# A recurrent-attention and FFT-gate kernel: hand-ordered chunk pipeline, natural-layout output, bonus summed on VectorE, half-length inverse, one PSUM ring

## The chip, the cores and the metric

The kernel runs on one core of a Trainium2 chip. Time is device microseconds (us) of one execution. Engines are named as in the profile: PE (TensorE matmul; PEld is its weight load), DVE (VectorE), ACT (ScalarE), POOL (GpSimd), SP (SyncE, which here only issues DMAs). SBUF and PSUM are the two on-chip memories in which the kernel keeps its tiles; its matmuls all write to PSUM tiles. The granted clock is the share of its full clock at which the profile shows PE running. Medians come from a few timed executions. Every run has a state, fast or slow.

## The reference, cut to what matters

Part one is a recurrence over 768 time steps for each of 4 batches and 8 heads of 48 channels. Part two projects its output, convolves one third of it with a filter by FFT, multiplies it by two gates and projects again.

```python
for t in range(S):                                    # S = 768, D = 48
    cur = einsum('bhd,bhe->bhde', u[None] * kt, vt)   # the "bonus"
    y[:, :, t] = einsum('bhd,bhde->bhe', rt, state + cur)
    state = wt[..., None] * state + einsum('bhd,bhe->bhde', kt, vt)
# x = y as (B, S, 384)
proj = x @ w_proj;  x1, x2, x3 = three parts of 384
x2_conv = irfft(rfft(x2, axis=1) * rfft(filter_fft, axis=0), n=S, axis=1)
return (x1 * x2_conv * x3) @ w_out
```

## The kernel before

Time is cut into chunks of 128 steps: 6 a batch, 24 in all. A chunk turns the recurrence into matmuls: cumulative sums of log decay (`csi`, `csT`), scaled keys `kh` and queries `qT`, scores `sc`, a masked score `mt`, the state, and the output `yT`, which is built channel-first. Two half sums `sd` of each pair of chunks (from chunk 3 of a batch on) feed the transform. The second stage of a batch (gates, transform, spectrum products, inverse, output projection) is a queue of closures, let in three at a time between the parts of later chunks. The framework's scheduler then orders each engine.

```python
# part_b: bonus on PE, from transposed r*k (tkT's second half)
for x, o in ((kh, 0), (rk, HP)):
    for j in range(HP):
        nc.tensor.transpose(tk[:, o + j, :], x[:, 2*j:2*j+2, :], ident)
nc.scalar.activation(out=tkT, in_=tk, func=AF.Copy)
...
nc.tensor.matmul(kv[:, C+2*j:C+2*j+2], tkT[:, HP+j, :], u_sb[:, j, :], ...)
...
nc.vector.tensor_copy(out=cc, in_=kv[:, C:])
nc.vector.tensor_mul(mt, sc..., mask)
nc.gpsimd.tensor_mul(vc, v_heads(vb), cc.to_broadcast(...))

# second stage: spectrum products on VectorE, six operations on 128x1152
def prods():
    nc.vector.tensor_mul(ua, xr, HR);  nc.vector.tensor_mul(ub, xi, HI)
    nc.vector.tensor_sub(pr, ua, ub)
    nc.vector.tensor_mul(ua, xr, HI);  nc.vector.tensor_mul(ub, xi, HG)
    nc.vector.tensor_add(pi, ua, ub)

# inverse: six full matmuls for each of 3 blocks x 2 halves
def inv(cb, hf):
    for n, q in enumerate((0, 2, 4, 1, 3, 5)):
        m = m2n[:, q-2, :] if (hf and q >= 2) else m2[:, q, :]
        nc.tensor.matmul(ps, P[q % 2][:, q//2, cb*L:(cb+1)*L], m, ...)
    nc.vector.tensor_mul(y[:, cb, sl], ps, g[:, cb, sl])
```

## Time and profile before

| | before |
|---|---|
| time, median | 222.61 us (221.51 to 223.82) |
| span of the profiled execution | 222.3 us |
| start to the first half sums | 48.8 us |
| three periods from batch to batch | 46.5, 46.4, 46.4 us |
| last first-half-sums to the end (tail) | 34 us |

The start time of the first half sums `sd` of each batch is the marker used all through; it cuts the run into a head, three periods and a tail. These lines are from the page of the profile: busy time by engine; in 40 slices the granted PE clock and the DMA share, in tenths; and the chain of work that ended last.

```profile
span 222.3 us, 4668 instructions
...
PE 181.1 (81%) x1778; PEld 123.3 (55%) x1778; DVE 143.8 (65%) x260; ACT 124.1 (56%) x233; POOL 81.6 (37%) x129
...
PEclk9999559699999999999999999999999999999998
DMA  6999999939598244995950709987401041000022
...
PE 53%; DVE 20%; ACT 12%; DMA 6%; issue 6%; SPq 1%; POOL 1%; DVEq 0%; ACTq 0%; POOLq 0%
```

No engine is full, and the chain passes through several. The same kernel by stretches of time (from and to, length, then busy time and instructions by engine, granted clock, DMA share, GB/s):

```profile
48.79:95.31 46.52, 41.72 (x437) 28.62 (x434) 32.81 (x53) 28.15 (x55) 18.74 (x29) 1.00 0.72 146
95.31:141.68 46.37, 41.55 (x437) 28.78 (x434) 32.30 (x54) 28.21 (x55) 18.07 (x29) 1.00 0.63 129
...
188.20:222.30 34.10, 25.14 (x193) 14.29 (x191) 15.19 (x28) 13.92 (x27) 2.45 (x3) 0.97 0.10 36
```

In a period DVE is busy 32 us of 46 (third pair of numbers), ACT 28, POOL 18. In the chain of waits (start, us, what), the head has one long piece:

```profile
10.52 11.23 DMA r_84<-in_r_dram
...
21.91 0.73 POOL rk_93 L321
22.86 0.84 POOL vc L364
```

POOL, which works in order, waits for chunk 2's `r` before it makes chunk 0's `vc`. Three groups by form (busy us, mean ns):

```profile
L490 DVE TENSOR_TENSOR y<-ps_i,g 128x384 bf16<-128x384 f32 x24 | 12.8, 555 | 16.5 <-PE ps_i L485 16.5
...
L456 DVE TENSOR_TENSOR sd_1437<-xT_841 128x384 bf16<-128x384 bf16 x3 | 3.4, 1127 | 1.7 <-ACT xT_841 L403 1.7
...
L456 DVE TENSOR_TENSOR sd_2907<-xT_2325 128x384 bf16<-128x384 bf16 x3 | 1.6, 521 | 2.7 <-ACT xT_2325 L403 2.7
```

The half sum has both inputs in SBUF and takes 1.13 us in batch 1, where POOL is at work, and 0.52 us in the last batch, where it nearly rests.

### The profile page before, as it was taken

Reading aid. Unit: us, or ns where it says so; the run is one execution under the profiler, and the core shown is the slowest. Engines: PE = TensorE matmul, PEld = TensorE weight load, DVE = VectorE, ACT = ScalarE, POOL = GpSimd, SP = SyncE. Lnnn points to the kernel's source line nnn. Section 1 sums busy time; section 2 is a strip of 40 time slices with the busy share of each in tenths; the row PEclk is TensorE's granted clock in tenths of the full one; section 3 lists DMA queues with packets and bytes.
Section 4 is the critical chain, followed back from the end, with each engine's and each line's share of the span. In section 5 each row is a group of like instructions: output and inputs, shape, how many; then the busy total and the mean of one; then the engine's idle time right before and its main releaser. Section 6 shows DMA issues by size and latency. Waiting matters only on the chain.

```text
span 222.3 us, 4668 instructions
## 1 busy us (share of the span) xinstructions
PE 181.1 (81%) x1778; PEld 123.3 (55%) x1778; DVE 143.8 (65%) x260; ACT 124.1 (56%) x233; POOL 81.6 (37%) x129
## 2 busy tenths in 40 slices
PE   0066797988798999978898999887979999779882
PEld 0054555766555657666465666665656666645341
DVE  8946366387759845776679384786696537734730
ACT  2396447467676346576773445767842475656022
POOL 8740366447312433463423235363232432400000
PEclk9999559699999999999999999999999999999998
DMA  6999999939598244995950709987401041000022
GB/s 132 175 307 229 282 166 193 182 66 198 108 192 158 56 85 100 257 179 112 174 108 2 143 19 278 173 170 137 79 3 35 0 147 69 4 0 0 3 106 108
DMA packets 105863, 27.44 MB, mean 123 GB/s; under 512 B 100464, under 2 KB 105456, under 8 KB 105840
## 3 DMA queue, kind: packets, MB, share of 16 engines
q1 hardware_dynamic: 105040, 25.96, 54.7%
q0 software_dynamic: 800, 1.18, 3.1%
q8 instruction: 14, 0.23, 0.5%
q14 instruction: 9, 0.07, 0.1%
HBM read 23.59 MB, written 4.72 MB: 127 GB/s over the span
## 4 chain that ended last, share of the span: by engine, by line
PE 53%; DVE 20%; ACT 12%; DMA 6%; issue 6%; SPq 1%; POOL 1%; DVEq 0%; ACTq 0%; POOLq 0%
PE yT L400 10%; PE ps_p L431 9%; PE ps_i L485 9%; DMA r_84<-in_r_dram 5%; PE ps_o L495 4%; DVE mt L362 4%; PE ps_f L254 3%; PE rT L317 3%; PE ps_f L246 3%; PE sc L355 3%; DVE g L443 2%; ACT tkT L337 2%; DVE sd_1437 L456 2%; DVE sd_2179 L456 2%; DVE sd_695 L456 2%
## 5 line engine op out<-in xcount | busy, mean ns | idle before, releaser
L362 DVE TENSOR_TENSOR mt<-sc,mask_excl 128x1024 bf16<-128x1024 f32 x24 | 29.2, 1216 | 1.1 <-PE sc L355 1.1
L337 ACT ACTIVATE tkT<-tk 128x1024 bf16<-128x1024 bf16 x24 | 24.6, 1023 | 1.4 <-PE tk L335 1.2
L490 DVE TENSOR_TENSOR y<-ps_i,g 128x384 bf16<-128x384 f32 x24 | 12.8, 555 | 16.5 <-PE ps_i L485 16.5
L431 PEld LDWEIGHTS <-wproj 128*128 128x128 bf16 x144 | 13.4, 99 | 14.1 <-issue 6.9
L499 ACT ACTIVATE o<-ps_o 128x384 f32<-128x384 f32 x24 | 11.4, 493 | 15.8 <-PE ps_o L495 15.8
L318 ACT ACTIVATE csi<-csi 128x384 f32<-128x384 f32 x24 | 11.6, 482 | 13.8 <-PE csi L310 13.8
L360 DVE COPY cc<-kv 128x8 f32<-128x8 f32 x24 | 3.9, 164 | 23.0 <-PE kv L347 22.8
L400 PE MATMUL yT<-ident,vc 128*128 128x128 bf16 x72 | 16.2, 225 | 2.2 <-POOL vc L364 2.2
L495 PE MATMUL ps_o<-wout,y 128*128 128x384 bf16 x72 | 15.2, 326 | 1.3 <-DVE y L490 0.7
L364 POOL TENSOR_TENSOR vc<-v_87,cc 128x384 bf16<-128x384 bf16 x8 | 6.6, 830 | 16.3 <-DVE cc L360 16.2
L272 PE MATMUL m2t<-ident,F 128*128 128x128 bf16 x18 | 2.8, 305 | 11.5 <-DVE ident L190 11.5
L324 DVE TENSOR_TENSOR qT<-rT,e_96 128x512 bf16<-128x512 f32 x12 | 8.2, 687 | 5.0 <-ACT e_96 L319 5.0
L355 PE MATMUL sc<-qT,tkT 48*128 48x128 bf16 x192 | 11.3, 223 | 0.0
L321 POOL TENSOR_TENSOR rk_93<-r_84,ld_k 128x384 bf16<-128x384 f32 x6 | 6.0, 999 | 13.1 <-PE tk L335 7.0
L400 PE MATMUL yT<-qT,st_98 128*128 128x128 bf16 x72 | 9.9, 219 | 0.7 <-DVE kh_91 L322 0.6
L368 POOL TENSOR_TENSOR phi<-e_95,blk 128x8 f32<-128x8 f32 x12 | 2.9, 244 | 20.4 <-ACT e_95 L319 17.3
L495 PEld LDWEIGHTS <-y 128*128 128x128 bf16 x72 | 6.6, 97 | 6.7 <-DVE y L490 1.9
L254 PE MATMUL ps_f<-ab,F 128*128 128x384 bf16 x48 | 9.7, 327 | 0.2
L400 PE MATMUL yT<-mt,v_87 128*128 128x128 bf16 x80 | 8.9, 219 | 1.1 <-DVE mt L362 1.1
L364 POOL TENSOR_TENSOR vc<-v_86,cc 128x384 bf16<-128x384 bf16 x8 | 6.6, 831 | 8.2 <-DVE cc L360 8.2
L400 PE MATMUL yT<-mt,v_88 128*128 128x128 bf16 x80 | 8.7, 225 | 0.8 <-DVE mt L362 0.8
L324 DVE TENSOR_TENSOR qT<-rT,e_95 128x512 bf16<-128x512 f32 x12 | 8.2, 684 | 1.4 <-ACT e_95 L319 1.2
(278 smaller groups left out, 538.4 us busy)
## 6 DMA issues: line engine op xcount, KB each, us to landing
ld_w<-in_w_dram SPq DMA_DIRECT2D x24, 192.0 KB, 3.9
ld_k<-in_k_dram SPq DMA_DIRECT2D x24, 192.0 KB, 3.2
ld_v<-in_v_dram SPq DMA_DIRECT2D x24, 192.0 KB, 4.2
out_dram<-o SPq DMA_DIRECT2D x3, 1152.0 KB, 5.2
filt<-in_moe_filter_fft_dram SPq DMA_DIRECT2D x2, 1152.0 KB, 8.2
r_82<-in_r_dram SPq DMA_DIRECT2D x6, 192.0 KB, 4.0
r_83<-in_r_dram SPq DMA_DIRECT2D x6, 192.0 KB, 3.6
r_84<-in_r_dram SPq DMA_DIRECT2D x6, 192.0 KB, 4.0
```

The source lines that it names most:

```text
L254: nc.tensor.matmul(ps, F[:, ti, c0:c0 + L], x[:, ti, :], start=(ti == 0), stop=(ti == NT - 1),)
L324: nc.vector.tensor_mul(qT, rT, e[:, :, 0:L])
L337: nc.scalar.activation(out=tkT, in_=tk, func=AF.Copy)
L355: nc.tensor.matmul(sc[:, par, j, :], tkT[p0:p0 + D, j, :], qT[p0:p0 + D, j, :], start=True, stop=True,)
L362: nc.vector.tensor_mul(mt, sc.rearrange("p q j t -> p (q j) t"), _mid(mask_excl, H))
L364: nc.gpsimd.tensor_mul(vc, v_heads(vb), cc.to_broadcast([L, H, D]))
L400: nc.tensor.matmul(yT[:, cb, :], lh, rh, start=(n == 0), stop=(n == len(ops) - 1))
L431: nc.tensor.matmul(ps, wproj[:, cb, col0:col0 + L], xT[:, cb, sl], start=(cb == 0), stop=(cb == CB - 1),)
L456: nc.vector.tensor_add(z(f"sd{0}")[:, :, sl], lo, hi)
L485: nc.tensor.matmul(ps, z(f"P{q % 2}")[:, q // 2, cb * L:(cb + 1) * L], m, start=(n == 0), stop=(n == 5),)
L490: nc.vector.tensor_mul(z("y")[:, cb, sl], ps, z("g")[:, cb, sl])
L495: nc.tensor.matmul(ps, z("y")[:, cb, ti * L:(ti + 1) * L], wout[:, cb, :], start=(cb == 0), stop=(cb == CB - 1),)
```

## The change

The intent: fewer and smaller matmuls, kept in an order made by hand. The bonus sum `cc` becomes a reduction on DVE of a product made by POOL; `kh` moves from DVE to POOL; the chunk's output is built time-first and then transposed; the inverse computes even and odd parts of half length, which DVE adds and subtracts; all PSUM tiles but the scores share one ring of six; the filter is loaded and transformed later.

```diff
+    def bonus_a(idx):
+        nc.gpsimd.tensor_mul(rk, r_bufs[idx % NR][:, :, 0:D], t["lk"])
+        nc.gpsimd.tensor_mul(t["rku"], rk, u_bc)
+        nc.gpsimd.tensor_copy(out=t["vb"], in_=t["lv"])
+    def bonus_b(idx):
+        nc.vector.tensor_reduce(out=cc, in_=t["rku"], axis=AX.X, op=ALU.add)
+        nc.gpsimd.tensor_mul(t["vc"], t["vb"], cc.to_broadcast([L, H, D]))
...
-        nc.vector.tensor_mul(kh[:, :, 0:D], lk, csi)
+        nc.gpsimd.tensor_mul(kh[:, :, 0:D], t["lk"], en)
...
-        def inv(cb, hf):            # 6 full matmuls, 6 times a batch
+        def inv(cb):                # 4 full, 4 half-row matmuls, 3 times
+            full = ((0, 0, 0, ev), (1, 1, 0, ev), (4, 0, 2, od), (5, 1, 2, od))
+            ...                     # first P0's, then P1's slices
+            nc.scalar.activation(out=ods, in_=od, func=AF.Copy)
+            nc.vector.tensor_add(eo[:, 0, :], ev, ods)
+            nc.vector.tensor_sub(eo[:, 1, :], ev, ods)
+            nc.vector.tensor_mul(z("y")[:, cb, :], eo..., z("g")[:, cb, :])
...
+    FILL = (2, 2, 2, 0)             # units of side work a chunk lets in
+    with tc.manual_schedule(engines={PE, Activation, DVE, Pool, SP}):
+        for idx in range(len(chunks)):
+            turn(idx)                          # transpose kh
+            begin(idx + 2); load_weights(idx); issue_loads(idx + 4)
+            fill(FILL[0])
+            scores(idx); decay(idx + 1); bonus_b(idx + 1); bonus_a(idx + 2)
+            fill(FILL[1])
+            output(idx)
+            fill(FILL[2])
+            turn_x(idx, xTs[b])                # transpose the output
...                                            # side work of batches 0 to 2:
+            ready[5] += fws + [F(prods, slice(0, 3))]
+            ready[5] += g1[0:4] + invs[0:1] + g1[4:6] + invs[1:3]
```

In the last batch the products are made in three slices between the transform's steps. The output steps of a batch are put into the queue in chunk 3 of the next. A unit is one queued step; an inverse block counts as two, the products and the half sums as none.

## The prediction

> **What bounds the kernel now.** No engine is full: the page has PE at 81% of 222.3 us, DVE 65%, ACT 56%, POOL 37%. The chain of waits gives PE 53%, DVE 20%, ACT 12%. I read three stages. (a) Head, to 48.8 us (first half-sums, group `sd`): the windows have the DMA share at about 1.0 until 40 us, and the chain has one wait of 11.2 us for chunk 2's `r`, because POOL's product for chunk 2 stands before chunk 0's `vc`. (b) Three batch periods of 46.4 us (`sd` at 48.8, 95.3, 141.7, 188.2). DVE is busy 32.5 us in each, ACT 28.1, POOL 18. PE reads 41.6, but that holds pipeline latency: in the timeline a run of six 384-column matmuls takes 1.14 us and one 0.33, so the step is 0.16 us; 128 columns 0.056, a concurrent half-row matmul 0.091, scores 0.025. With these steps a batch needs about 37 us of PE, 79% of the period; the rest is hand-offs (score, mask, `yT`, `xT`, `sd` in turn on the chain). (c) Tail, 34 us, of which 25 follow the last chunk.
>
> **Costs of the change, per batch.**
> PE: the inverse goes from 36 full matmuls to 12 full and 12 concurrent halves: 5.8 to 3.0 us. A chunk drops four `rk` transposes, four bonus products, and 19 `yT` steps of 0.056 us for 13 mostly small ones, and adds three transposes and one identity product: 2.75 to about 2.25 us. Together 37 to about 31 us.
> DVE: `kh` (0.55 us a chunk) goes to POOL, `cc` (0.16) becomes a reduction over 384 elements, which I estimate at 0.55. The Trainium skill ("VectorE: DVE Perf Modes", the perf-mode tier table) gives a reduction only the plain rate, like the 0.55 us of the 384-element tensor-tensors here. The inverse's six 0.55 us become six of 0.55 and three of about 0.55: +1.7. Net about +1: 33 to 36.5 us.
> ACT: the key transpose halves (1.02 to about 0.59), `xn` adds 0.49, `ods` 1.5 a batch: about 32 us.
> POOL: about 4.4 us a chunk instead of 3.4.
> The skill ("SBUF — State Buffer", on the shared port pair) says a two-input VectorE operation from SBUF waits for a GpSimd operation reading SBUF. The trace agrees: `sd` takes 1.13 us on average in busy batches, 0.52 in the last. More POOL work keeps that cost.
>
> So the bound moves to DVE, 36-37 us a batch. PE's saving (6 us) counts only because the order made by hand lets hand-offs overlap.
>
> **On the critical path.** Batch period 46.4 to about 41 (DVE near 88%): about 16 us over three. Head: POOL's wait goes, the 3.7 us of zeroing before the masks go, the filter load moves back; but chunk loads (about 4.7 us of all DMA engines each) still pace it: 4-6 us. Tail: shorter inverse, products by slice, outputs after: about 6 us; the last inverse's chain (copy, add, subtract, multiply, about 2.2 us) gives some back.
>
> **Predicted: 193 us**, 184 to 204 in 8 of 10. Faster by over 2%: 0.94; within: 0.04; slower: 0.02.
>
> **What would show it.** DVE's busy share near 75%, PE's falling to about 75% with about 1490 matmuls; POOL above 50%; batch period 40-42 us; no DMA wait over 5 us on POOL in the head; inverse matmuls about 1 us a block; half-sums not faster than before.
>
> **What would make it wrong.** ACT, issuing in order, waits for a late `w` load before the chunk's own work, so the head stays DMA-paced; key product on POOL (1 us, late) holds the transposes; DVE blocked longer by POOL; one PSUM ring of six holding PE. Then 200-210. If hand-offs vanish and DVE runs above 93%: 182.

## The result and the profile after

The changed kernel took 204.02 us (median of 202.74 to 206.22), beside 223.22 us for the kernel before in the same rounds. The ratio, 0.913 with a 95% interval of 0.904 to 0.922, is the mean time of the one kernel's fast runs over that of the other's of the same rounds, so it is not quite the ratio of the medians. All ratios below are made that way against the kernel before. The result lies at the very end of the stated range (184 to 204), 11 us above the number predicted.

| | before | predicted | after |
|---|---|---|---|
| start to first half sums | 48.8 us | 43 to 45 | 39.7 us |
| periods | 46.5, 46.4, 46.4 | 41 each | 46.7, 40.8, 40.9 us |
| tail | 34 | 28 | 34.7 us |

The page of the changed kernel, as above:

```profile
span 202.9 us, 4168 instructions
...
PE 156.5 (77%) x1490; PEld 97.7 (48%) x1490; DVE 153.6 (76%) x249; ACT 126.5 (62%) x269; POOL 121.6 (60%) x162
...
PEclk9999696996999969999999799999997999999678
DMA  6999989799987871833989928339930000140024
...
DVE 31%; PE 25%; issue 12%; ACT 12%; DMA 8%; SPq 6%; POOL 4%; DVEq 0%; ACTq 0%; POOLq 0%
```

DVE now leads the chain. The granted clock has a dip in every batch and a long one at the end, which the kernel before did not have after its head. By stretches:

```profile
39.70:86.45 46.75, 37.73 (x388) 23.98 (x387) 41.42 (x57) 30.17 (x67) 33.26 (x39) 0.93 0.85 150
86.45:127.26 40.81, 35.27 (x363) 22.36 (x362) 36.67 (x51) 28.48 (x65) 29.75 (x37) 0.96 0.73 146
...
168.16:202.90 34.74, 26.11 (x171) 12.86 (x169) 19.33 (x44) 17.38 (x38) 3.02 (x5) 0.89 0.19 69
```

DVE is busy 36.7 us of 40.8, POOL 29.7 where it was 18. The groups that answer to those shown of before:

```profile
L483 DVE TENSOR_TENSOR y<-eo,g 128x768 bf16<-128x768 bf16 x12 | 14.0, 1164 | 0.4
...
L436 DVE TENSOR_TENSOR sd_1353<-xT_866 128x384 bf16<-128x384 bf16 x3 | 2.9, 962 | 0.0
...
L435 DVE TENSOR_TENSOR sd_1351<-xT_866 128x384 bf16<-128x384 bf16 x3 | 1.6, 523 | 2.0 <-ACT xT_866 L385 2.0
```

The new gate product `y` has both inputs in SBUF. The 1.16 us is a mean over all twelve: the three of the last batch, where POOL is idle, take 0.56 us each, and the nine of the other batches 1.28 to 1.41, 1.37 on average.

The most telling view is the timeline of one batch (start us, us, engine, line, what; in brackets the idle time before it and what ended it). These lines are cut out of the stretch from 103 to 115 us:

```profile
103.07 1.23 DVE L343 TENSOR_TENSOR mt<-sc,mask_excl 128x1024 bf16<-128x1024 f32 x1 [1.99 <-PE sc L338]
...
105.81 0.75 DVE L455 TENSOR_TENSOR U_1805<-X_1684,HR 128x1152 bf16<-128x1152 bf16 x1
106.47 1.39 DVE L456 TENSOR_TENSOR U_1806<-X_1690,HI 128x1152 bf16<-128x1152 bf16 x1
107.21 1.51 POOL L280 TENSOR_TENSOR rk<-r_76,ld_k 128x384 bf16<-128x384 f32 x1
107.89 1.44 DVE L457 TENSOR_TENSOR P_1803<-U_1805,U_1806 128x1152 bf16<-128x1152 bf16 x1
108.80 1.32 POOL L281 TENSOR_TENSOR rku<-rk,u_bc 128x384 bf16<-128x384 bf16 x1
109.37 1.36 DVE L458 TENSOR_TENSOR U_1805<-X_1684,HI 128x1152 bf16<-128x1152 bf16 x1
110.65 1.05 DVE L459 TENSOR_TENSOR U_1806<-X_1690,HG 128x1152 bf16<-128x1152 bf16 x1
111.06 1.50 POOL L312 TENSOR_TENSOR kh_84<-ld_k,en 128x384 bf16<-128x384 f32 x1
111.74 1.43 DVE L460 TENSOR_TENSOR P_1804<-U_1805,U_1806 128x1152 bf16<-128x1152 bf16 x1
...
113.23 0.34 PE L467 MATMUL ps_e<-m_171,P_1804 128*128 128x384 bf16 x1 [3.19 <-DVE P_1804 L460]
...
114.02 1.21 DVE L343 TENSOR_TENSOR mt<-sc,mask_excl 128x1024 bf16<-128x1024 f32 x1
```

The six products stand as one block of 7.4 us on DVE (105.81 to 113.17). The next chunk's scores were ready at 108.5, but its mask product `mt` comes 10.9 us after the one before it; other chunks of this batch need 4.7 to 7.8 us. DVE is busy for 10.84 us of this step, so here it is the limit, though it is not over the whole period. PE, also in order, waits 3.2 us at the inverse for the last product. The kernel before spent 5.5 us on the same six operations in a middle batch and 4.5 us in its last, with POOL idle. POOL is slowed as well: beside the block its `rk`, `rku` and `kh` products take 1.51, 1.32 and 1.50 us, in the chunk before 1.00, 0.93 and 1.01.

### The profile page after: what moved, and what is told of

Read it like the earlier page. It is cut to its first block, busy times and chain, and to the rows that moved or that the text cites. A ratio compares the mean times of both kernels' runs of the same rounds, so it can differ in the third digit from the quotient of the medians.

```text
span 202.9 us, 4168 instructions
## 1 busy us (share of the span) xinstructions
PE 156.5 (77%) x1490; PEld 97.7 (48%) x1490; DVE 153.6 (76%) x249; ACT 126.5 (62%) x269; POOL 121.6 (60%) x162
## 3 DMA queue, kind: packets, MB, share of 16 engines
HBM read 22.61 MB, written 4.72 MB: 135 GB/s over the span
## 4 chain that ended last, share of the span: by engine, by line
DVE 31%; PE 25%; issue 12%; ACT 12%; DMA 8%; SPq 6%; POOL 4%; DVEq 0%; ACTq 0%; POOLq 0%
DMA ld_w<-in_w_dram 8%; DVE mt L343 6%; PE ps_p L415 4%; PE ps_o L490 4%; DVE g L427 4%; ACT tkT L326 3%; PE yn L371 2%; DVE cc L290 2%; SPq L91 2%; ACT ab L445 2%; PE sc L338 2%; DVE eo L481 2%; DVE eo L482 2%; DVE qT L316 2%; ACT o L494 2%
## 5 line engine op out<-in xcount | busy, mean ns | idle before, releaser
L291 POOL TENSOR_TENSOR vc<-v,cc 128x384 bf16<-128x384 bf16 x24 | 21.9, 912 | 34.6 <-PE yt L384 16.5
L343 DVE TENSOR_TENSOR mt<-sc,mask_excl 128x1024 bf16<-128x1024 f32 x24 | 29.2, 1215 | 12.4 <-PE sc L338 12.4
L281 POOL TENSOR_TENSOR rku<-rk,u_bc 128x384 bf16<-128x384 bf16 x24 | 24.4, 1019 | 1.9
L376 ACT ACTIVATE xn<-yn 128x384 bf16<-128x384 f32 x24 | 11.8, 490 | 14.5 <-PE yn L371 13.8
L312 POOL TENSOR_TENSOR kh_83<-ld_k,en 128x384 bf16<-128x384 f32 x12 | 12.0, 1000 | 14.4 <-ACT en L310 14.2
L310 ACT ACTIVATE en<-csi 128x384 f32<-128x384 f32 x24 | 11.9, 497 | 8.7 <-PE csi L301 7.4
L326 ACT ACTIVATE tkT<-tk 128x512 bf16<-128x512 bf16 x24 | 14.4, 598 | 2.1 <-PE tk L324 2.1
L290 DVE TENSOR_REDUCE cc<-rku 128x8 f32<-128x384 bf16 x24 | 13.0, 541 | 2.9 <-POOL rku L281 2.9
L282 POOL CAST v<-ld_v 128x384 bf16<-128x384 f32 x24 | 14.4, 602 | 0.0
L483 DVE TENSOR_TENSOR y<-eo,g 128x768 bf16<-128x768 bf16 x12 | 14.0, 1164 | 0.4
L312 POOL TENSOR_TENSOR kh_84<-ld_k,en 128x384 bf16<-128x384 f32 x12 | 13.8, 1148 | 0.2
L371 PE MATMUL yn<-v,mt 128*128 128x48 bf16 x192 | 9.7, 192 | 5.1 <-DVE mt L343 5.1
```

The source lines that it names most:

```text
L281: nc.gpsimd.tensor_mul(t["rku"], rk, u_bc)
L282: nc.gpsimd.tensor_copy(out=t["vb"], in_=t["lv"])
L290: nc.vector.tensor_reduce(out=cc, in_=t["rku"], axis=AX.X, op=ALU.add)
L291: nc.gpsimd.tensor_mul(t["vc"], t["vb"], cc.to_broadcast([L, H, D]))
L312: nc.gpsimd.tensor_mul(kh[:, :, 0:D], t["lk"], en)
L343: nc.vector.tensor_mul(mt, sc.rearrange("p q j t -> p (q j) t"), _mid(mask_excl, H))
```

## The experiments

All twelve runs started from the changed kernel. Except where said, they are correct. Four theories came up in turn. Theory 1, mine at first: DVE's total work, swollen by POOL, bounds the period. Theory 2: PE does. Theory 3: the block of products on DVE, in order, holds the chunk behind it. Theory 4: PE's wait at the inverse does.

### The hand order given up

```diff
-    with tc.manual_schedule(engines={ENG.PE, ENG.Activation, ENG.DVE, ENG.Pool, ENG.SP}):
+    if True:
```

> The changed kernel with the hand order given up (all engines ordered by the framework's scheduler), nothing else. If the gain of the change comes mainly from the order: 213 us or more, batch period back to 44 to 46 us. If it comes mainly from the smaller PE work: within 2% of 204 us.

Measured: 197.39 us, ratio 0.888 (0.879 to 0.897), which lies below the changed kernel's interval. Neither expectation holds: without the hand order the same instructions are 3% faster. Two periods and the tail of this variant:

```profile
86.71:125.34 38.63, 35.19 (x366) 22.37 (x365) 32.91 (x53) 28.30 (x64) 29.93 (x38) 0.96 0.79 160
125.34:162.88 37.54, 33.21 (x355) 21.23 (x353) 31.86 (x50) 27.46 (x62) 22.54 (x30) 1.00 0.40 89
162.88:194.60 31.72, 24.23 (x184) 13.27 (x182) 17.48 (x43) 17.33 (x38) 1.17 (x2) 0.95 0.21 75
```

DVE is busy 33 instead of 37 us a period. In this timeline two gate products stand among the six spectrum products, and these sum to 6.5 us. So the gain of the change does not come from its order; the rest of the change, in the scheduler's order, gives more. Which part of the rest gives it is not separated by this run. It is the best correct kernel.

### The full inverse back

```diff
-            full = ((0, 0, 0, ev), (1, 1, 0, ev), (4, 0, 2, od), (5, 1, 2, od)) ...
+            for n, q in enumerate((0, 2, 4, 1, 3, 5)): ...   # as before, 6 blocks
+            nc.vector.tensor_mul(z("y")[:, cb, sl], ps, z("g")[:, cb, sl])
```

> The changed kernel with the inverse of before: 36 full matmuls a batch instead of 12 full and 12 halves, one VectorE product per block straight from PSUM, no ScalarE copy. PE +2.8 us a batch; VectorE: six products of 0.55 us in place of six of 0.55 us and three that measured 1.2 us with GpSimd busy, so -3.8 us; ScalarE -1.5 us. Theory 1 (VectorE bounds the batch period, 36.7 of 40.8 us busy): period about 38 us, total 194 to 199 us. Theory 2 (PE bounds it, or its waits behind the products do): period 42 to 43 us, total 209 to 213 us.

Measured: 200.75 us, ratio 0.903 (0.897 to 0.908). One period and the tail:

```profile
85.13:125.63 40.50, 37.43 (x376) 24.63 (x375) 33.91 (x47) 27.09 (x61) 28.92 (x37) 0.96 0.83 147
...
166.55:198.80 32.25, 26.48 (x208) 15.69 (x206) 17.79 (x41) 17.22 (x37) 2.86 (x5) 1.00 0.21 74
```

DVE has 2.8 us less to do in the period and PE 2.2 us more, and the period is as long as before, 40.5 us. Theories 1 and 2 both fall as they stand: neither engine's total alone sets it. Since the edit trades DVE work for PE work, it does not show that less DVE work by itself would bring nothing. (The 1.2 us in the expectation is the mean over all batches; the busy ones take 1.37.) The half-length inverse bought nothing in the middle of this order; the intervals overlap the changed kernel's by a little, so its whole effect on the time is not clear of noise. In the profiled runs the tail is 2.5 us shorter with the full inverse, at a clock of 1.00 instead of 0.89.

### The bonus back on PE

```diff
-        nc.gpsimd.tensor_mul(t["rku"], rk, u_bc)
-        nc.vector.tensor_reduce(out=cc, in_=t["rku"], axis=AX.X, op=ALU.add)
+        # 4 transposes of rk, one ACT copy rkT, 4 two-column matmuls with u_sb
+        nc.vector.tensor_copy(out=cc, in_=pc)
```

> The changed kernel with the bonus sum back on PE (four transposes of rk and four two-column products a chunk, one ScalarE copy more), so that VectorE has a 0.16 us copy for the 0.54 us reduction and GpSimd loses one 1.0 us product a chunk. VectorE -2.3 us a batch, GpSimd -6 us, PE +1.9 us, ScalarE +3.5 us. Theory 1 (VectorE with GpSimd holding it up): period 37.5 to 39 us, and the six spectrum products together below 7 us instead of 7.4; total 195 to 200 us. Theory 2 (PE bounds): period 42 us or more, 208 us or more.

Measured: 201.70 us, ratio 0.907 (0.902 to 0.913); periods 40.3 and 40.5 us, with DVE 31.7 us busy and PE 37.7. The products sum to 6.7 us and the long chunk step is 9.9 us instead of 10.9. Five us less DVE work a period brought 0.4 to 0.5 us; neither expectation holds. I had counted on 2.3 us less; DVE's own operations also became shorter with POOL busy for 6.5 us less (the six half sums after batch 1's marker sum to 2.9 us instead of 4.5). Here too PE got more work, 2.4 us, and ACT 3.1. The block's step became 1.0 us shorter and another one as well, and a third grew by 1.2 us.

### The tail kept warm

```diff
-            ready[5] += [F(prods, slice(2, 3))] + g1[4:6] + invs
+            ready[5] += [F(prods, slice(2, 3))] + g1[4:6]
+            ready[5] += [F(warm, 10)] + invs + [F(warm, 14)]   # matmuls of no use
```

> The changed kernel with 10 matmuls of no use before the last batch's inverse and 14 before its output projections, where PE waits for VectorE. If the half clock that the profile shows from 188 us on costs the tail what its matmuls lost (18 output matmuls at 0.28 us instead of 0.16, and three inverse blocks at about 1.9 us instead of 1.6): 2 to 3 us less than the changed kernel, so about 201 us. If the tail hangs on VectorE and ScalarE alone: no difference.

The changed kernel's own tail, two stretches, and the same of this one:

```profile
190.00:195.00 5.00, 3.32 (x16) 0.94 (x13) 3.88 (x8) 0.98 (x2) 0.00 (x0) 0.79 0.00 0
195.00:199.50 4.50, 4.22 (x16) 1.85 (x14) 0.00 (x0) 2.70 (x6) 0.00 (x0) 0.62 0.49 175
```

```profile
190.00:195.00 5.00, 5.00 (x34) 2.30 (x32) 4.29 (x9) 1.47 (x3) 0.00 (x0) 1.00 0.02 3
```

Measured: 201.16 us. The ratio is 0.903 (0.896 to 0.910); the interval overlaps the changed kernel's, so the time alone would not settle it. In the changed kernel's tail these are the waits of PE before its clock falls, at about 188.7 us:

```profile
186.74 0.34 PE L467 MATMUL ps_o<-m_171,P_3021 128*128 128x384 bf16 x1 [1.36 <-DVE P_3021 L457]
187.80 0.34 PE L467 MATMUL ps_o<-m_171,P_3022 128*128 128x384 bf16 x1 [0.72 <-DVE P_3022 L460]
```

The profiled run is a slow one, so only its tail is used: it is 32.4 us long (169.63 to 202.0) against 34.7. A run made for another purpose agrees: the spread products, next, leave the last batch as the changed kernel has it, with the same 171 matmuls in the tail, but kept a clock of 0.99 there, and their tail is 32.3 us. The short products, the last experiment, stand between: the same 171 matmuls, clock 0.93, 33.8 us. So the low clock costs 2.4 us of the tail. The Trainium skill ("TensorE: Matmul & The Clock Gate", section "Why this matters for your kernels") advises against idle gaps of over about 3 us; here no gap in this stretch was that long. The longest PE wait in the four us before the clock fell was 1.36 us, with single matmuls between the waits.

### The products spread

```diff
-            ready[5] += fws + [F(prods, slice(0, 3))]
-            ready[5] += g1[0:4] + invs[0:1] + g1[4:6] + invs[1:3]
+            ready[5] += fws
+            for n in range(6):
+                ready[5] += [F(prods, slice(0, 3), (n,)), g1[n]]
+            ready[5] += invs
```

> The changed kernel in its own hand order, except that in batches 0 to 2 the six spectrum products no longer stand on VectorE as one block of 7.4 us: each is followed by one gate step, and the inverse comes after all six gates. Same instructions, same counts. Theory 3 (formed from the last four runs: the batch period is a sum of chunk steps, and the longest one, 10.9 us from mask product to mask product, is the in-order wait behind the block): that step falls to 8 us or less, batch period 37 to 39 us, total 195 to 199 us. Theory 1 (VectorE's total work bounds the period): period stays at 40 to 41 us, total 202 to 205 us.

Measured: 205.82 us, ratio 0.925 (0.919 to 0.931); periods 42.7 and 41.9 us. The first chunk step falls from 10.9 to 8.0 us, as expected, and the next grows from 7.8 to 12.4 us (11.6 in the other batches):

```profile
111.49 1.21 DVE L343 TENSOR_TENSOR mt<-sc,mask_excl 128x1024 bf16<-128x1024 f32 x1
...
116.24 0.50 PE L470 MATMUL ps_e<-m,P 128*128 128x384 bf16 x1 [2.95 <-DVE P L463]
...
123.90 1.21 DVE L343 TENSOR_TENSOR mt<-sc,mask_excl 128x1024 bf16<-128x1024 f32 x1
```

PE still reaches the inverse before the last product, and now the inverse stands before the next chunk's transposes and scores, so DVE runs dry in turn. Moving the block's parts apart moved the wait. The expected time failed; Theory 3 in its simple form, with the mask product as the only thing held, is not enough.

### The filter later

```diff
-        if n == 1:          # load the filter
+        if n == 3:
...
-                if idx == 3:   # queue its transform
+                if idx == 5:
```

> The changed kernel with the filter loaded in chunk 3 instead of chunk 1 and its spectrum made from chunk 5 instead of chunk 3 on. If the head is held by the queue of loads, in which the 1.15 MB filter stands before chunk 5's w (a 5.2 us wait on ScalarE at 31 us): the wait goes, and the first long stretch, from the start to batch 1's first half sums at 86.5 us, ends 2 to 4 us earlier; total 200 to 202 us. If all loads together bound the first 57 us: no change or a new wait later.

Measured: 207.14 us, ratio 0.931 (0.924 to 0.938), slower. The first long stretch does end 4.9 us earlier (first half sums of batch 1 at 81.6 instead of 86.5 us), but periods two and three are 41.8 and 41.9 us, and the tail is this:

```profile
165.32:204.30 38.98, 28.18 (x200) 14.96 (x197) 22.40 (x51) 19.59 (x41) 3.03 (x5) 0.94 0.17 61
```

The tail holds 200 matmuls where the changed kernel's holds 171. A count of the queue in the program says why this can be: six units of side work are let in a chunk, and none are saved up. With the filter's six units queued two chunks later, chunks 3 and 4 have too little to do, and 34 units instead of 28 are left after the last chunk. What was won at the head was given back at the end.

### The full inverse with spread products

This is the full inverse and the spread products together, edits as above.

> The full inverse of before together with the spread products. Theory 3 says the full inverse brought nothing to the batch period (40.5 to 40.9 us, as the changed kernel) because the block of products ruled it; with the block gone VectorE's 3 us less a batch should now show: period 36 to 38 us, total 191 to 196 us, faster than the spread products alone. If PE is the next bound (37.5 us busy of 40.5 us): period 38.5 to 39.5 us, no better than the spread products alone.

Measured: 202.62 us, ratio 0.908 (0.900 to 0.916); periods 41.3 and 40.3 us. Expectations of either kind fail for the periods. The total is no better than the full inverse alone, but it is better than the spread products alone (0.925), by 1.4 and 1.6 us a period. So with the block spread the full inverse does bring something: what the same exchange is worth changes with the order.

### The full inverse in the automatic order

The edits of the first and the second experiment together.

> The automatically ordered variant, which took 197.4 us, with the full inverse of before. Its period was 37.5 to 38.6 us with VectorE 33 us busy. If VectorE or the hand-offs through the inverse's four steps bound it: 193 to 196 us. If PE: 198 us or more.

Measured: 205.18 us, ratio 0.920 (0.913 to 0.927); periods 43.6, 42.4 and 39.3 us. This is the outcome "PE", but its PE is busy 37.7 us of 42.4, DVE only 29.7, and the granted clock of that period is 0.92. In this order the half-length inverse is worth over 3%, in the hand order nothing that is clear of noise. The scheduler's order is no recipe either: the same rule that gave 197 us for one inverse gave 205 for the other.

### The outputs put between

```diff
-            ready[5] += g1[0:4] + invs[0:1] + g1[4:6] + invs[1:3]
+            ready[5] += g1 + prev_outs + invs     # outputs of the batch before
```

> The changed kernel in its hand order, but the six output steps of the batch before are held back and put between the products and the inverse, for batches 1 and 2, so that PE has other work in front of the inverse until the products are done. Theory 4 (PE, in order, stands at the inverse's second matmul for the last product, 3.2 us a batch, and the next chunk's transposes, scores and mask product stand behind it): that wait disappears, VectorE does its backlog meanwhile, periods of batches 2 and 3 fall from 40.8 to 37.5 to 39 us; total 197 to 200 us. Theory 1 (VectorE's work with GpSimd's hold-ups, 36.7 us, plus hand-offs it can't avoid): the wait only moves to the mask product, periods stay at 40 to 41 us.

Measured: 208.62 us, ratio 0.936 (0.932 to 0.941); periods 40.2 and 42.4 us, tail 37.2 us with 199 matmuls in it instead of 171. PE's wait at the inverse is gone from the list of waits, as Theory 4 wanted, and the long step stays at 10.9 us. PE now waits elsewhere:

```profile
113.23 0.50 PE L363 MATMUL yn<-vc,ident 128*128 128x384 bf16 x1 [2.84 <-DVE g L427]
```

The chunk's output tile `yn` waits for a gate product, with which it shares nothing but the PSUM ring; I read this as its slot coming free only then. The gate product stands behind the block of products on DVE. So Theory 4 falls as the only cause, and the ring looks like one more way in which the block holds PE; no run here took the ring apart.

### The filter later, with seven units a chunk

```diff
-    FILL = (2, 2, 2, 0)
+    FILL = (2, 2, 3, 0)
```

> The late filter once more, with seven instead of six units of side work let in per chunk. The late filter brought the first batch 4.9 us forward but the tail came out 4.3 us longer. My reading is that six units a chunk is a quota: side work that had no turn early is left for the tail (a count of the queue gives 34 units left after the last chunk against 28). If so, with seven units the count is 26, and the tail is back at 34 us or below while the periods grow by less than 0.7 us: total 199 to 202 us. If the longer tail had another cause, it stays at 38 to 39 us and the total at 205 us or more.

Measured: 211.25 us, ratio 0.948 (0.943 to 0.953). The tail came back to 35.4 us with 186 matmuls. I had expected 34 us or below, so the queue explains most of the longer tail and not all of it; and the periods grew to 49.9, 42.4 and 43.5 us, by far more than the 0.7 us I allowed. Letting more in is not free when it shifts what stands behind what.

### All three

> Outputs between, late filter with seven units, and the warm tail of the earlier run together. If the three act in different places (periods, head and backlog, tail) they add up: 202.9 less about 5, 3 and 2.5, so 191 to 195 us, faster than the automatically ordered variant at 197.4 us. If one takes the other's room, for example seven units undoing the gap in front of the inverse: 197 us or more.

Measured: 215.13 us, ratio 0.964 (0.958 to 0.971). The three do not add up; they take each other's room. The periods are 49.6, 44.7 and 47.5 us. The edits are those of the outputs between, the later filter with seven units, and the warm tail.

### The block of products cut short (wrong)

```diff
+            if b < B - 1:
+                nc.vector.tensor_mul(pr, xr, HR[:, sl, :])
+                nc.vector.tensor_mul(pi, xi, HI[:, sl, :])
+                return
```

> The changed kernel, with only two of the six spectrum products in batches 0 to 2 (the last batch keeps all): a wrong result on purpose, to see what the block itself costs. VectorE loses about 5 us of 7.4 us in each of three batches, all of it in one place. If the block stands with its whole length on the path of the batch period (the chunk's mask product, the gates' PSUM slots and the inverse all wait behind it): the 10.9 us step falls to about 6 us, periods of batches 2 and 3 from 40.8 us to 36 to 37 us, total 189 to 193 us. If the period has another chain beside it, as the full inverse suggests, where 3 us less VectorE work elsewhere brought nothing: periods 39 us or more, total 198 us or more. The tail should not move.

Measured: 188.96 us, ratio 0.849 (0.839 to 0.859), with a wrong result (relative error 0.87), as meant. The same stretch as shown of the changed kernel, and one period:

```profile
99.20 1.23 DVE L343 TENSOR_TENSOR mt<-sc,mask_excl 128x1024 bf16<-128x1024 f32 x1 [1.99 <-PE sc L338]
...
101.94 0.75 DVE L456 TENSOR_TENSOR P<-X,HR 128x1152 bf16<-128x1152 bf16 x1
102.61 1.38 DVE L457 TENSOR_TENSOR P<-X,HI 128x1152 bf16<-128x1152 bf16 x1
...
105.40 1.22 DVE L343 TENSOR_TENSOR mt<-sc,mask_excl 128x1024 bf16<-128x1024 f32 x1
```

```profile
82.59:118.52 35.93, 33.56 (x363) 21.92 (x362) 31.43 (x47) 28.42 (x65) 27.77 (x37) 1.00 0.84 166
```

The step falls from 10.9 to 6.2 us and the period from 40.8 to 35.9, with all 363 matmuls still there and the clock at 1.00. DVE lost 5.2 us of work and the period 4.9. The tail, which should not have moved, is 33.8 us instead of 34.7, with the clock at 0.93 instead of 0.89. These are the six steps from mask product to mask product (us) of one period, in order, from the timelines:

| | | | the block's | | | |
|---|---|---|---|---|---|---|
| changed kernel | 5.39 | 4.71 | 10.95 | 7.75 | 7.06 | 4.94 |
| full inverse | 5.36 | 4.51 | 10.95 | 6.83 | 7.03 | 5.83 |
| bonus on PE | 5.59 | 5.93 | 9.95 | 7.63 | 6.09 | 5.10 |
| short products | 5.39 | 4.72 | 6.20 | 7.63 | 7.06 | 4.94 |

With the short products only the block's step changes. The step after it, in which the changed kernel's clock is 0.81 on average, becomes 0.12 us shorter, so the clock is not what shortened the period. Where the full inverse took 2.8 us from DVE and the bonus 5.0 without moving the period by more than 0.5, these 5.2 us count almost in full. Work in the block is on the path. That the same amount elsewhere on DVE is not is shown only for the two exchanges made here, in which another engine got more to do.

## Why the prediction was right or wrong

- **Counts and shares: right.** PE has 1490 matmuls as predicted, DVE 76% (about 75 predicted), PE 77% (about 75), POOL 60% (above 50). A full-clock inverse block is about 1 us, and the half sums did not get faster (1.49 us a pair in batch 1, before 1.47). The reduction takes 0.54 us on average for its 384 elements, as the Trainium skill ("VectorE: DVE Perf Modes", the perf-mode tier table) let me expect: it gives a reduction only the plain rate.
- **Periods two and three: right in size, wrong in cause.** 40.8 and 40.9 us against "about 41", with DVE at 36.7 us. I wrote "the bound moves to DVE". DVE's 36.7 us agree with the 36.5 I wrote by luck: my terms (33 and about 1) sum to 34, and what lifts the sum above that is mainly two costs that I had left out, given in the next point but one. DVE is the limit in the block's step, not over the period. The full inverse and the bonus on PE take 2.8 and 5.0 us from DVE and the period stays at 40.3 to 40.9 us; the short products take 5.2 us and it falls by 4.9. So where the work stands matters more than how much it is: a 7.4 us block in front of the next chunk's mask product, the gates' products and the inverse, on engines that work in order.
- **"The order made by hand lets hand-offs overlap": failed.** The scheduler's order of the same instructions is faster, 197.4 us.
- **DVE's costs: one term mis-sized, one left out.** I took 0.55 us for the inverse's last product; it measured 1.37 us where POOL is busy and 0.56 where it is not, which is 2.5 us more a batch. The Trainium skill ("SBUF — State Buffer", the section on who interferes with whom) says that a DVE operation with two SBUF inputs contends with a GpSimd operation that reads SBUF. I cited this for the half sums and did not apply it to the new operation or to the six products (7.4 us against 5.5 in the kernel before, 1.9 us more). Both were in my list of what would make the prediction wrong ("DVE blocked longer by POOL"), for which I gave 200 to 210 us. ACT's 32 us was too high; it measured 28.5.
- **Head: right in sum, wrong in split.** The first half sums came 9.1 us earlier, not 4 to 6, but the first period is 46.7 us. The filter's transform moved into it (its first matmuls on the chain are at 45.6 us, before at 28.6), and DVE is busy 41.4 us there; I read this as the reason. A 5.2 us wait of ACT for `w`, which I had listed as a danger, came too, but in the head (31 to 36 us). Head and first period together gained 8.9 us; I had 10.4 (5 and 5.4), so the sum is near because two errors are opposite.
- **Tail: the term that made most of the miss.** I predicted 28 us, and it is 34.7, as long as before. Of the 6.7 us, 2.4 are the low clock (the warm tail, and the spread products with the same tail at a clock of 0.99). The tail also begins with work that was not in the old one: batch 2's six output steps, 18 matmuls of 0.163 us, run from 171 to 175 us, after the marker, while the kernel before had ended them at 180 us, before its marker at 188. That is 2.9 us of PE; that the tail is longer by it is a count and was not tested. I compared tails by their last batch and forgot the queue. The remaining 1.4 us are not explained.

In sum: my three terms promised 16, 5 and 6, that is 27 us, and the spans show 19.4 us (222.3 to 202.9). The difference of 7.6 us is, within rounding, 6.6 us that the tail missed and 1.5 us of head and first period, less 0.4 us that periods two and three gained more than I said. The other two to three us of the miss are my own arithmetic: 222.6 less 27 is 195.6, and I wrote 193.

Still open: which part of the change brings its 9% (the order does not, and two of its parts, the half-length inverse and the bonus on DVE, can be put back in the hand order without loss; the time-first output, `kh` on POOL, the PSUM ring and the later filter were not tried one by one); why each order gives the period it does (spreading the block, filling the gap at the inverse and letting in more units all made it longer); whether spread products together with outputs between would remove both waits; and how much of the block's growth from 5.5 to 7.4 us POOL causes: the timelines show the operations of both engines stretched side by side, but no run kept POOL away from the block.

## What to carry to other kernels

Before you price a saving by an engine's busy share, find the longest step between two instances of the same instruction and see what stands in it: microseconds inside that block counted almost in full here, and microseconds moved from elsewhere on the same engine to another engine counted for nearly nothing. An order made by hand is a claim to be tested against the scheduler's, with the same instructions. When side work runs from a queue with a quota, count what is left at the end; a gain at the start can come back as a longer tail.

## What the Trainium skill lacked or had wrong

- "TensorE: Matmul & The Clock Gate" (section "Why this matters for your kernels") warns of PE gaps over about 3 us. In this case's tail the clock fell, to 0.79 and then 0.62 of full on average over the stretches shown, with no PE wait longer than 1.36 us in the four microseconds before; between the waits of 1.36 and 0.72 us stood single matmuls. It cost 2.4 us of 34.7. So the table's rule is not enough by itself. The page does not lack the case: its section "A second HAM failure mode: psum-queue depth-cycling" has the clock oscillate where PE often idles briefly between groups of matmuls. It gives no share of idle time for it.
- "SBUF — State Buffer" (who interferes with whom) gives the rule that a two-input DVE operation contends with a GpSimd read, and the traces agree in direction. It gives no size for a stream of small operations: here 128x768 products took 1.37 us instead of 0.56, and POOL at 60% rather than 37% went with 7.4 instead of 5.5 us for the six 128x1152 products.
- On a shared ring of PSUM tiles the skill has only a general remark ("Perfetto Trace Analysis", section "Optimization Strategy": repeated gaps can mean that there is no room for the next tile). I found no page that says that a ring can tie two stages to each other. In the run with the outputs between, PE stood 2.8 us at the chunk's output, ended by a gate product of another stage; that the ring is the reason is my reading.
